# Decoding the last weights inside the last product of a three-layer kernel, and adding one product straight from PSUM

## The chip, the cores and the metric

The kernel runs on one core of one Trainium2 chip. The core has five engines that each run their own program in order: TensorE (PE, matmuls), VectorE (DVE), ScalarE (ACT), GpSimd (POOL) and SyncE (SP), which here only issues transfers (DMA). They meet at semaphores. The metric is the device time of one execution in microseconds (us), the median of three runs; lower is better.

## The reference

All data are fp32. An attention with a small memory is followed by two layers on 2304 tokens of 512 values:

```
a    = softmax(phi, over the sequence)                    # 32 memory rows per head
k_m, v_m = a^T k, a^T v
attn = softmax(q k_m^T / sqrt(64)) v_m                    # 4 batches, 8 heads, 576 x 64
x    = attn as 2304 x 512
x    = ((x @ w_a) * (x @ w_b)) @ w_out                    # 512 -> 1536 -> 512
h    = x @ moe2_w_in                                      # 512 -> 2048
out  = (h * sigmoid(1.702 h)) @ moe2_w_out                # 2048 -> 512
```

## The kernel before

**Numbers.** A product in full fp32 is made of three passes of a faster form: each operand is split into a high part (a copy to fp32r, on ACT, L281) and the rest (a subtraction on POOL or DVE, L275), by `hi_lo`; the passes are high x high, low x high, high x low.

**Weights arrive as 64-bit numbers** and are decoded on the chip. Sixteen pieces of `w_in` and sixteen chunks of `w_out` of the last layer, 128 rows of 512 values each, come as raw words of 512 KB into one of two buffers `raw` (L307). `decode_piece` makes one step on ACT (`Abs`, L379), a maximum on DVE or POOL (L381) and three steps on DVE (L385, L389, L394) into one of the decode buffers `dm`; the last of them gives the raw buffer back, and SP may then load the next piece into it. DVE reads the raw words in the last two steps.

**The last layer's first product** is computed by seven products instead of eight (P1 to P7, each on sums and differences of quarters of the operands) for each of 24 pairs of a group of 256 features `g` (8) and a group of 768 tokens `p` (3). The code calls such a pair a `quad`. One product is 6 matmuls of 128x384 (L1046) into one of eight PSUM banks. The results are put together in the SBUF tile `acc`: P1 and P5 are copied there by ACT (`kept`, L1081), P6, P2, P7, P3 and P4 are added from PSUM by DVE to something in `acc` (`added`, L1088), and two sums that hold P5 are made from two SBUF tiles by POOL or DVE (`paired`, L275). The four blocks that come out go through the gelu on ACT (L1105) and are written to DRAM, `g2d` (L1107).

**The last product** (`proj2`, L1174) has 18 token tiles of 128, each with 16 chunks of the contraction and three passes: 864 matmuls of 128x512. It reads the gelu's results back, 384 tokens and half of the contraction at a time (`load_gated`, L1139, 1536 KB), splits them into tiles `sb`, and sums a token tile over two halves of 8 chunks in one bank. The weights for it are chunks decoded between the quads, written to DRAM as fp32 (`w2d`, L408), read back when there is room for their split form (`load_chunk`, L1120) and split then (`split_chunk`).

**What sets the order.** `Order` runs all these generators against simulated clocks of the four engines, with a price for each operation, a priority for each stream and a model of the transfers, and so writes one fixed program for each engine; SP's program is in the order in which the generators issue transfers. Pieces are decoded in the order of the list `pieces`: two pieces of `w_in` per feature group and, from the third group on, three chunks of `w_out` behind them. At run time each engine follows its program, and an instruction that waits holds up all that stand behind it on its engine.

## Time and profile before

| | us |
|---|---|
| median of 3 runs | 840.15 (839.57 to 840.37) |
| the profiled execution, as a run | 842.18 |
| its span in the trace | 840.4 |
| PE busy | 801.4 |
| DVE busy | 554.4 |
| ACT busy | 396.3 |
| POOL busy | 345.3 |

The mean granted clock of TensorE was 0.942 of 2.4 GHz. In the trace the attention lies in the first 100 us, the middle layer runs from there to about 434, the quads of the last layer from about 415 to 636, and the last product from 636 to 835.7. A row of a window gives an engine's busy time in a stretch and, in brackets, the number of its instructions; a row of a group gives count, busy time and mean duration of one form of instruction, then how long the engine stood idle ahead of such instructions and what ended that. A timeline row has the idle time ahead of an instruction in square brackets, with what ended it.

### The profile page before, as it was taken

To read this page: it belongs to the slowest core of one execution; us is meant where nothing else is said; L and a number is where in the kernel's file an instruction comes from. 1 tells how busy PE (TensorE), PEld (TensorE's weight loads), DVE (VectorE), ACT (ScalarE), POOL (GpSimd) and SP (SyncE) were. 2 spreads that over 40 slices of the span, in tenths; PEclk is the share of its full clock that TensorE was granted. 3 is DMA by queue.
4 is the path that set the end of the run, shared out by engine and by line. 5 is a ranking of instruction groups with operands and counts; after the bars stand their busy time and mean duration, and the time that the engine had idled before them with its cause. 6 is when DMAs were issued, how large, how long until landed. Compare 5 with 4: busy or idle time off the path is not lost. (4 is left out here: it accounts for less than half of the span.)

```text
span 840.4 us, 13393 instructions
## 1 busy us (share of the span) xinstructions
PE 801.4 (95%) x4928; PEld 706.5 (84%) x4928; DVE 554.4 (66%) x965; ACT 396.3 (47%) x863; POOL 345.3 (41%) x327
## 2 busy tenths in 40 slices
PE   8989999989999999999988898788999999999997
PEld 7768888889889999999887897777998888888886
DVE  4979879997978778648999778689665212222120
ACT  4567767454555445426564445444574322222210
POOL 1314244653546335226998777567555000000000
PEclk9999999999999999999898999899999999999999
DMA  8776302321311303000124446776469523343201
GB/s 307 264 232 192 99 1 76 101 76 51 100 52 51 101 2 100 25 2 1 60 92 130 155 151 218 258 241 214 150 218 317 180 91 109 105 159 114 90 23 37
DMA packets 63937, 103.89 MB, mean 124 GB/s; under 512 B 5760, under 2 KB 42624, under 8 KB 63872
## 3 DMA queue, kind: packets, MB, share of 16 engines
q1 hardware_dynamic: 63040, 102.23, 37.4%
q10 hardware_dynamic: 832, 0.82, 0.3%
q8 instruction: 38, 0.62, 0.3%
q14 instruction: 27, 0.22, 0.1%
HBM read 75.24 MB, written 27.79 MB: 123 GB/s over the span
## 5 line engine op out<-in xcount | busy, mean ns | idle before, releaser
L275 DVE TENSOR_TENSOR attn<-acc,attn 128x1024 fp32r<-128x1024 f32 (+1 forms) x41 | 49.4, 1208 | 125.3 <-ACT attn L281 125.3
L1174 PE MATMUL bank<-y,attn 128*128 128x512 f32 x540 | 127.8, 394 | 0.0
L1174 PEld LDWEIGHTS bank<-y,attn 128*128 128x128 f32 x540 | 101.7, 188 | 23.0
L275 POOL TENSOR_TENSOR acc<-acc 128x384 f32<-128x384 f32 (+1 forms) x64 | 76.1, 1196 | 48.4 <-DVE acc L1088 21.3
L281 ACT ACTIVATE attn<-acc 128x1024 fp32r<-128x1024 f32 (+1 forms) x48 | 43.5, 920 | 66.2 <-PE bank L1174 59.2
L1088 DVE TENSOR_TENSOR acc<-bank,acc 128x384 f32<-128x384 f32 x120 | 63.4, 548 | 12.8 <-ACT acc L1081 5.9
L1105 ACT ACTIVATE acc<-acc 128x384 f32<-128x384 f32 x96 | 46.9, 517 | 43.0 <-DVE acc L1088 39.4
L275 POOL TENSOR_TENSOR y<-gr,y 128x288 fp32r<-128x288 f32 x43 | 37.5, 871 | 70.8 <-ACT y L281 70.7
L800 DVE TENSOR_TENSOR gr<-bank,gr 128x288 f32<-128x288 f32 x96 | 43.1, 450 | 30.8 <-PE bank L784 23.1
L797 ACT ACTIVATE gr<-bank 128x288 f32<-128x288 f32 x96 | 38.1, 399 | 39.6 <-PE bank L784 35.4
L817 PE MATMUL bank<-g,whl_b 128*128 128x288 f32 x384 | 53.7, 296 | 3.2 <-POOL g L275 2.1
L784 PE MATMUL bank<-attn,eff 128*128 128x288 f32 x384 | 55.1, 297 | 1.0 <-ACT eff L755 0.7
L817 PEld LDWEIGHTS bank<-g,whl_b 128*128 128x128 f32 x384 | 51.8, 188 | 4.5 <-POOL g L275 2.6
L379 ACT ACTIVATE dm<-raw 128x512 f32<-128x512 f32 x51 | 33.8, 671 | 45.9 <-DMA raw<-in_moe_w_in_dram 18.2
L784 PEld LDWEIGHTS bank<-attn,eff 128*128 128x128 f32 x384 | 52.2, 188 | 3.1 <-issue 1.0
L275 POOL TENSOR_TENSOR g<-gr,g 128x288 fp32r<-128x288 f32 x37 | 35.4, 962 | 44.2 <-ACT g L281 44.2
L840 PE MATMUL bank<-y,whl_a 128*128 128x512 f32 (+1 forms) x240 | 52.2, 371 | 0.4 <-POOL y L275 0.4
L840 PEld LDWEIGHTS bank<-y,whl_a 128*128 128x128 f32 x240 | 41.6, 188 | 9.3 <-POOL y L275 1.2
L394 DVE SCALAR_TENSOR_TENSOR dm<-raw,dm 128x512 uint32<-128x512 uint32 x49 | 45.2, 922 | 0.3
L389 DVE SCALAR_TENSOR_TENSOR dm<-raw,dm 128x512 uint32<-128x512 uint32 x51 | 43.9, 860 | 0.5
L275 POOL TENSOR_TENSOR wab_hl<-dm,wab_hl 128x512 fp32r<-128x512 f32 (+1 forms) x30 | 34.2, 1148 | 22.8 <-ACT wab_hl L281 20.5
L784 PE MATMUL bank<-attn,eff_b 128*128 128x288 f32 x288 | 40.8, 296 | 1.3 <-DVE acc L871 1.1
(241 smaller groups left out, 1809.4 us busy)
## 6 DMA issues: line engine op xcount, KB each, us to landing
g2d<-acc SPq DMA_DIRECT2D x96, 192.0 KB, 3.2
acc<-g2d SPq DMA_DIRECT2D x12, 1536.0 KB, 6.6
raw<-in_moe_w_out_dram SPq DMA_DIRECT2D x28, 512.0 KB, 3.9
raw<-in_moe_w_in_dram SPq DMA_DIRECT2D x16, 512.0 KB, 4.2
raw<-in_moe_w_a_dram SPq DMA_DIRECT2D x20, 256.0 KB, 2.9
raw<-in_moe_w_b_dram SPq DMA_DIRECT2D x20, 256.0 KB, 3.1
q<-in_q_dram SPq DMA_DIRECT2D x8, 576.0 KB, 6.7
out_dram<-dm SPq DMA_DIRECT2D x56, 64.0 KB, 1.7
```

The lines of the kernel that those rows point to most:

```text
L275: (nc.gpsimd if e == POOL else nc.vector).tensor_tensor(out=dst, in0=in0, in1=in1, op=op)
L281: nc.scalar.activation(out=hi, in_=src, func=AF.Copy)
L389: nc.vector.scalar_tensor_tensor(out=mu, in0=hw, scalar=0xC0000000, in1=mu, op0=ALU.bitwise_and, op1=ALU.bitwise_or)
L394: nc.vector.scalar_tensor_tensor(out=dst.bitcast(U32), in0=lw, scalar=29, in1=mu, op0=ALU.logical_shift_right, op1=ALU.bitwise_or)
L784: nc.tensor.matmul(ps[0][:, :U], e[c][:, sw, i * CW + j * P:i * CW + (j + 1) * P], attn(b, mv, c, u * U, U), start=(n == 0), stop=(n == 3 ...
L797: nc.scalar.activation(out=gr[0], in_=pa_[0][:, :U], func=AF.Copy)
L800: nc.vector.tensor_tensor(out=gr[0], in0=pb[0][:, :U], in1=gr[0], op=ALU.mult)
L817: nc.tensor.matmul(ps[0][:, :U], w[:, sw, j, mb * P:(mb + 1) * P], g1[0][:, j, mv, :], start=(n == 0), stop=(n == 3 * G1 - 1),)
L840: nc.tensor.matmul(ps[0][:, :e - o], w[:, sw, j, mb * P:(mb + 1) * P], g1_all[mv][:, j, o:e], start=(n == 0), stop=(n == 3 * G1 - 1),)
L1088: nc.vector.tensor_tensor(out=s[0], in0=ps[0][:, :N2], in1=x[0], op=ALU.add)
L1105: nc.scalar.activation(out=c[0], in_=c[0], func=AF.Gelu_apprx_sigmoid)
L1174: nc.tensor.matmul(ps[s][0], b[0][:, sw, c, :], wo2[h * KH + c][:, mv], start=(h == c == n == 0), stop=(h == 1 and c == KH - 1 and n == 2),)
```

## The change

- **P5 is not copied.** The quad's order becomes P1, P6, P7, P5, P3, P4, P2, and DVE adds P5 from its bank twice, to two tiles of `acc`; `paired` is gone. Per quad ACT has one copy instead of two, DVE seven sums from PSUM instead of five, and the sums of two SBUF tiles fall away.
- **No way through DRAM for the last weights.** The sixteen chunks of `w_out` stand behind all pieces of `w_in` in the list, and `decode_piece` splits a chunk straight into its place once there is room. `w2d`, its 16 writes and 16 reads are gone. Eight chunks are decoded in the last quads, eight within the last product.
- **More decode buffers.** Two views of a tile that the attention no longer uses serve as decode buffers for the first three pieces of `w_in` (`BRIEF`) beside the one already there, and are retired before that memory is used anew.
- **The last product.** Its first two units of 384 tokens (`FRONT`; six token tiles) go by quarters of the contraction: chunks 0 to 3 for all six tiles, then 4 to 7, and so on, with six banks open; the others by halves as before. Tiles `sb` have 8 places instead of 4.

Counted in DVE's program from the first sum of the quads to the last:

| on DVE | before | after |
|---|---|---|
| sums from PSUM (L1088, after L1104) | 120 | 168 |
| decodes (their last three steps) | 27 | 18 |
| of these with the maximum on DVE | 22 | 10 |
| splits of 128x384 | 22 | 18 |
| splits of 128x256 | 14 | 1 |
| the same within the first four quads: sums / decodes / splits of 128x384 | 20 / 6 / 21 | 28 / 2 / 18 |

```diff
+    bdv_m = p2.tile([P, B * H * M], F32, name="bdv")
+    bdv = [
+        bdv_m[:, b * H * M:(b + 1) * H * M].rearrange("p (r m) -> p r m", r=H // 2) for b in range(B)
+    ]
     gr_s = slots(p2, 3, [P, U], "gr")
-    dm_x = slots(p2, 1, [P, 512], "dm_x").free[0]
-    dm_s.free.append(dm_x)
+    dm_x = slots(p2, 1, [P, 512], "dm_x").free
+    dm_s.free += dm_x
...
-    chunks = [(("o2", c), 0, [rows(w_o2, c, 1, 0, DM)], 1) for c in range(F2 // P)]
     for g in range(NG2):
         pieces += [(("in", g), i, [rows(w_in, 2 * i, 2, g * G2 * P, G2 * P)], 2) for i in range(2)]
-        for _ in range(3 if g > 1 else 0):
-            if chunks:
-                pieces.append(chunks.pop(0))
-    pieces += chunks
+    pieces += [(("o2", c), 0, [rows(w_o2, c, 1, 0, DM)], 1) for c in range(F2 // P)]
...
-            if m is dm_x and name[0] in ("in", "o2"):
-                od.mark(m[1], "dm_x")
-                m = yield "slot", dm_s
-            if name[0] == "in" and name[1] < 2:
+            if name[0] in ("in", "o2"):
+                brief, aside = (name, part) in BRIEF, []
+                while any(m is x for x in dm_x) != brief:
+                    aside.append(m)
+                    m = yield "slot", dm_s
+                dm_s.free += aside
+            if name[0] == "in" and name[1] < 3:
                 prio = PI
             elif name[0] in ("in", "o2"):
                 prio = PR
             od.spawn(prio, decode_piece(max(t, m[1]), i, name, part, n, m))
+
+    BRIEF = ((("in", 0), 0), (("in", 0), 1), (("in", 1), 0))
+
+    def retire_dm(m, t):
+        if any(m is x for x in dm_x):
+            od.mark(t, "dm_x", len(retired))
+            retired.append(m)
+        else:
+            dm_s.release(m, t)
+
+    retired = []
...
         elif name[0] == "o2":
             c = name[1]
-            nc.sync.dma_start(out=w2d[c * P:(c + 1) * P, :], in_=m[0])
-            dm_s.release(m, t + 2500.0)
-            od.mark(t + 2500.0, *name)
+            t = max(t, (yield "mark", "room", *name))
+            t = yield from hi_lo(t, wo2[c][:, HI], wo2[c][:, LO], m[0], DM)
+            dm_s.release(m, t)
+            od.mark(t, "wo2", c)
         else:
...
+        more = [[bdv_m[:, i * 512:(i + 1) * 512], t1] for i in range(2)]
+        dm_x.extend(more)
+        dm_s.free += more
...
+    def room_split(*flat):
+        give(sb_s, [x.rearrange("p (i c t) -> p i c t", i=2, c=KH) for x in flat])
...
+        room_split(*views(big["wab"], SN, 2), big["vhl"], spare())
...
+        if name == "P1":
+            od.spawn(0, kept(t, q, ps, "s"))
+        left = [len(SUMS[name])]
+        for other, out_, place in SUMS[name]:
+            od.spawn(0, added(t, q, ps, other, out_, place, left))
 
     SUMS = {
-        "P1": ("s", None, None), "P5": ("p5", None, None), "P6": ("u2", "s", None), "P2": ("c11", "s", (0, 0)),
-        "P7": ("u3", "u2", None), "P3": ("c12", "u4", (0, 1)), "P4": ("c21", "u3", (1, 0)),
+        "P1": (), "P6": (("s", "u2", None),), "P7": (("u2", "u3", None),),
+        "P5": (("u2", "u4", None), ("u3", "c22", (1, 1))), "P3": (("u4", "c12", (0, 1)),),
+        "P4": (("u3", "c21", (1, 0)),), "P2": (("s", "c11", (0, 0)),),
     }
-    USES = {"s": 2, "p5": 2, "u2": 2, "u3": 2, "u4": 1}
+    USES = {"s": 2, "u2": 2, "u3": 2, "u4": 1}
...
+    def added(t, q, ps, other, name, place, left):
         t1, x = yield from get(q, other)
         t, s = yield DVE, max(t, t1), dve(N2), hb_s
         nc.vector.tensor_tensor(out=s[0], in0=ps[0][:, :N2], in1=x[0], op=ALU.add)
-        bank_m.release(ps, t)
+        left[0] -= 1
+        if left[0] == 0:
+            bank_m.release(ps, t)
         drop(q, other, t)
-        yield from put(t, q, name, s, place)
-
-    def paired(q, one, two, name, place=None):
-        t1, x = yield from get(q, one)
-        t2, y = yield from get(q, two)
-        s = yield "slot", hb_s
-        t = yield from combine(max(t1, t2, s[1]), s[0], x[0], y[0], ALU.add, N2)
-        drop(q, one, t)
-        drop(q, two, t)
...
+    FRONT = 2
+    parts = [(i, h) for h in range(2) for i in range(FRONT)]
+    parts += [(i, h) for i in range(FRONT, len(units)) for h in range(2)]
...
+        for i, h in parts:
+            for g in range(h * n, (h + 1) * n):
+                for j in range(2):
+                    t = yield "mark", "g2", (g, i // 2), j, i % 2
+            s = yield "slot", f_s
+            f = s[0].rearrange("p (c t) -> p c t", c=KH)
+            o = units[i]
...
+    def proj2(tiles, cuts):
+
+        ps = {}
+        for o, e in cuts:
+            h = o // KH
+            for i, s in tiles:
                 t = yield "mark", "sb", i, h, s
-                if i == s == 0:
-                    for c in range(h * KH, (h + 1) * KH):
-                        t = max(t, (yield "mark", "wo2", c))
-                b = loaded.pop(("sb", i, h, s))
-                if h == 0:
-                    t, ps[s] = yield PE, t, 680 * KH, bank_m
+                for c in range(o, e):
+                    t = max(t, (yield "mark", "wo2", c))
+                b = loaded["sb", i, h, s]
+                if o == 0:
+                    t, ps[i, s] = yield PE, t, 680 * (e - o), bank_m
                 else:
-                    t, _ = yield PE, t, 680 * KH
-                for c in range(KH):
+                    t, _ = yield PE, t, 680 * (e - o)
+                for c in range(o, e):
                     for n, (mv, sw) in enumerate(PASSES):
                         nc.tensor.matmul(
-                            ps[s][0], b[0][:, sw, c, :], wo2[h * KH + c][:, mv],
-                            start=(h == c == n == 0), stop=(h == 1 and c == KH - 1 and n == 2),
+                            ps[i, s][0], b[0][:, sw, c - h * KH, :], wo2[c][:, mv],
+                            start=(c == n == 0), stop=(c == 2 * KH - 1 and n == 2),
                         )
-                sb_s.release(b, t)
-                if h == 1:
-                    od.spawn(0, proj2_out(t, units[i] // P + s, ps[s]))
+                if e % KH == 0:
+                    sb_s.release(b, t)
+                if e == 2 * KH:
+                    od.spawn(0, proj2_out(t, units[i] // P + s, ps[i, s]))
...
+        for i in range(3):
+            yield "mark", "dm_x", i
         room_projected()
         od.spawn(6, load_gated())
         od.spawn(5, split_gated())
-        for c in range(F2 // P):
-            od.spawn(6, load_chunk(c))
         for q in order[1:]:
             yield from quad(*q)
             if q == (NG2 - 1, 0):
                 room_chunks(*views(big["y0"], CN, 10))
             if q == (NG2 - 1, 1):
-                room_split()
+                room_split(*views(attn_m[0], SN, 2), *views(attn_m[1], SN, 2))
...
+        tiles = [(i, s) for i in range(len(units)) for s in range(N2 // P)]
+        n = FRONT * N2 // P
+        yield from proj2(tiles[:n], [(o, o + KH // 2) for o in range(0, 2 * KH, KH // 2)])
+        for o in range(n, len(tiles), N2 // P):
+            yield from proj2(tiles[o:o + N2 // P], [(0, KH), (KH, 2 * KH)])
 
     def quad(g, p):
-        for name in ("P1", "P5", "P6", "P2", "P7", "P3", "P4"):
+        for name in ("P1", "P6", "P7", "P5", "P3", "P4", "P2"):
```

In the orders below names are those of buffers, with the number of a tile behind some of them; line numbers of the changed kernel are its own (L1081 is L1097 there, L1088 L1104, L1105 L1114, L1107 L1116, L307 L308, L379 to L394 L390 to L405). DVE within the second and third quad before:

```order
L1088 TENSOR_TENSOR acc<-bank_76,acc 128x384
L381 TENSOR_SCALAR dm_85<-dm_85 128x512
L1088 TENSOR_TENSOR acc<-bank_71,acc 128x384
L385 TENSOR_SCALAR dm_85<-dm_85 128x512
L389 SCALAR_TENSOR_TENSOR dm_85<-raw_79,dm_85 128x512
L1088 TENSOR_TENSOR acc<-bank_74,acc 128x384
L275 TENSOR_TENSOR eff_b<-acc,eff_b 128x384
L394 SCALAR_TENSOR_TENSOR dm_85<-raw_79,dm_85 128x512
L381 TENSOR_SCALAR dm_83<-dm_83 128x512
L275 TENSOR_TENSOR g_95<-acc,whl_b 128x384
L385 TENSOR_SCALAR dm_83<-dm_83 128x512
```

and after:

```order
L1104 TENSOR_TENSOR acc<-bank_72,acc 128x384 x2
L1104 TENSOR_TENSOR acc<-bank_71,acc 128x384
L276 TENSOR_TENSOR whl_b<-acc,whl_b 128x384
L1104 TENSOR_TENSOR acc<-bank_70,acc 128x384
L276 TENSOR_TENSOR g_94<-acc,g_94 128x384
L1104 TENSOR_TENSOR acc<-bank_73,acc 128x384
L276 TENSOR_TENSOR g_94<-acc,g_94 128x384 x2
L276 TENSOR_TENSOR rest<-acc,rest 128x384
L1104 TENSOR_TENSOR acc<-bank_76,acc 128x384
L276 TENSOR_TENSOR rest<-acc,g_94 128x384
L1104 TENSOR_TENSOR acc<-bank_74,acc 128x384
```

The steps of two decodes (L381 to L394) stood between the sums; now sums and splits (L275, after L276) alternate.

ACT in the middle of the quads, before:

```order
L1081 ACTIVATE acc<-bank_75 128x384
L1081 ACTIVATE acc<-bank_77 128x384
L379 ACTIVATE dm_84<-raw_80 128x512
L1105 ACTIVATE acc<-acc 128x384
L379 ACTIVATE acc<-raw_79 128x512
L1105 ACTIVATE acc<-acc 128x384 x3
L1081 ACTIVATE acc<-bank_78 128x384
L1081 ACTIVATE acc<-bank_75 128x384
L379 ACTIVATE dm_83<-raw_80 128x512
L1105 ACTIVATE acc<-acc 128x384
L379 ACTIVATE dm_85<-raw_79 128x512
```

and after:

```order
L282 ACTIVATE wab_hl<-dm_82 128x256
L1114 ACTIVATE acc<-acc 128x384
L282 ACTIVATE wab_hl<-dm_82 128x256
L1114 ACTIVATE acc<-acc 128x384
L282 ACTIVATE wab_hl<-dm_83 128x256
L1114 ACTIVATE acc<-acc 128x384 x2
L1097 ACTIVATE acc<-bank_77 128x384
L390 ACTIVATE dm_82<-raw_79 128x512
L390 ACTIVATE dm_83<-raw_78 128x512
L1114 ACTIVATE acc<-acc 128x384 x4
L1097 ACTIVATE acc<-bank_73 128x384
```

Steps of a decode (L379) came every one to four instructions, between copies (L1081) and gelus (L1105). Now two of them (L390) stand together, and no others for a group's worth of gelus and splits (L282).

SP in the middle of the quads, before:

```order
L1107 DMA g2d<-acc 128x384 x3
L408 DMA w2d<-dm_85 128x512
L307 DMA raw_79<-in_moe_w_out_dram 128x1024
L1107 DMA g2d<-acc 128x384
L408 DMA w2d<-dm_84 128x512
L307 DMA raw_80<-in_moe_w_in_dram 128x2x512
L1107 DMA g2d<-acc 128x384 x3
L1139 DMA acc<-g2d 128x8x384
L408 DMA w2d<-dm_85 128x512
L307 DMA raw_79<-in_moe_w_in_dram 128x2x512
L1107 DMA g2d<-acc 128x384
```

and after:

```order
L1116 DMA g2d<-acc 128x384
L308 DMA raw_79<-in_moe_w_in_dram 128x2x512
L1116 DMA g2d<-acc 128x384 x3
L308 DMA raw_78<-in_moe_w_in_dram 128x2x512
L1116 DMA g2d<-acc 128x384 x9
L308 DMA raw_79<-in_moe_w_out_dram 128x1024
L1116 DMA g2d<-acc 128x384 x3
L308 DMA raw_78<-in_moe_w_out_dram 128x1024
L1116 DMA g2d<-acc 128x384 x9
L308 DMA raw_79<-in_moe_w_out_dram 128x1024
L1116 DMA g2d<-acc 128x384 x3
L308 DMA raw_78<-in_moe_w_out_dram 128x1024
```

A load of raw words stood behind a write of a decoded chunk (L408); now it stands among the gelu's writes to `g2d` alone.

## Rows read from the trace of the kernel before

**Rows 1.** The page, busy time of engines (us, share of span, instructions)
```profile
PE 801.4 (95%) x4928; PEld 706.5 (84%) x4928; DVE 554.4 (66%) x965; ACT 396.3 (47%) x863; POOL 345.3 (41%) x327
```

**Rows 2.** Windows: length, busy us and count of PE, PEld, DVE, ACT, POOL; clock, DMA
```profile
406.10:470.00 63.90, 54.95 (x294) 50.26 (x293) 63.34 (x94) 33.26 (x73) 57.71 (x50) 0.88 0.36 113
470.00:605.40 135.40, 121.37 (x640) 110.48 (x638) 101.45 (x170) 67.01 (x154) 90.64 (x88) 0.94 0.60 201
605.40:636.00 30.60, 30.59 (x175) 30.60 (x176) 20.66 (x30) 20.97 (x42) 20.15 (x17) 0.95 0.69 222
636.00:835.70 199.70, 199.65 (x865) 162.28 (x863) 45.69 (x38) 48.75 (x60) 8.12 (x6) 0.95 0.37 120
```

**Rows 3.** Windows, line L1046 alone: length, PE, PEld, clock, DMA share, GB/s
```profile
406.10:470.00 63.90, 41.80 (x196) 37.44 (x197) 0.88 0.36 113
470.00:605.40 135.40, 121.37 (x640) 110.48 (x638) 0.94 0.60 201
605.40:636.00 30.60, 30.59 (x174) 30.30 (x174) 0.95 0.69 222
```

**Rows 4.** Groups of instructions, PE, 406.1 to 470: count, busy us, mean ns, idle before
```profile
L817 PE MATMUL bank<-g,whl_b 128*128 128x288 f32 x50 | 7.5, 299 | 2.1 <-POOL g L275 2.1
L784 PE MATMUL bank<-attn,eff_b 128*128 128x288 f32 x48 | 6.5, 294 | 0.0
```

**Rows 5.** Groups of instructions, DVE, 406 to 636
```profile
L1088 DVE TENSOR_TENSOR acc<-bank,acc 128x384 f32<-128x384 f32 x118 | 62.4, 548 | 10.9 <-ACT acc L1081 5.9 <-ACT y L281 2.6 <-PE bank L1046 1.8
L394 DVE SCALAR_TENSOR_TENSOR dm<-raw,dm 128x512 uint32<-128x512 uint32 x22 | 21.0, 953 | 0.1
L389 DVE SCALAR_TENSOR_TENSOR dm<-raw,dm 128x512 uint32<-128x512 uint32 x21 | 19.3, 918 | 0.2
L385 DVE TENSOR_SCALAR dm<-dm 128x512 uint32<-128x512 uint32 x21 | 13.7, 652 | 4.0 <-POOL dm L381 3.6
L381 DVE TENSOR_SCALAR dm<-dm 128x512 f32<-128x512 f32 x19 | 13.2, 697 | 14.3 <-ACT dm L379 13.9 <-POOL vhl L275 0.4
L275 DVE TENSOR_TENSOR attn<-acc,attn 128x384 fp32r<-128x384 f32 x7 | 7.9, 1128 | 0.0
L275 DVE TENSOR_TENSOR wab_hl<-dm,wab_hl 128x256 fp32r<-128x256 f32 x4 | 2.8, 704 | 1.2 <-ACT wab_hl L281 1.2
```

**Rows 6.** Groups of instructions, ACT, 406 to 636
```profile
L1081 ACT ACTIVATE acc<-bank 128x384 f32<-128x384 f32 x48 | 21.9, 477 | 2.1 <-POOL y L275 1.6 <-PE bank L1046 0.5
L379 ACT ACTIVATE dm<-raw 128x512 f32<-128x512 f32 x20 | 13.3, 666 | 28.5 <-DMA raw<-in_moe_w_in_dram 18.2 <-DMA raw<-in_moe_w_out_dram 10.2
```

**Rows 7.** Groups of instructions, POOL, 406 to 636
```profile
L275 POOL TENSOR_TENSOR acc<-acc 128x384 f32<-128x384 f32 x57 | 68.3, 1204 | 48.4 <-DVE acc L1088 21.3 <-issue 16.4 <-ACT acc L1081 6.1
L381 POOL TENSOR_SCALAR acc<-acc 128x512 f32<-128x512 f32 x3 | 5.2, 1722 | 0.7 <-DVE dm L394 0.6
```

**Rows 8.** Timeline of ACT: start, us, engine, line, operation [idle before]
```profile
499.88 0.66 ACT L379 ACTIVATE dm<-raw 128x512 f32<-128x512 f32 x1 [3.90 <-DMA raw<-in_moe_w_out_dram]
500.44 0.51 ACT L1105 ACTIVATE acc<-acc 128x384 f32<-128x384 f32 x1
```

**Rows 9.** Timeline of PE
```profile
501.98 1.33 PE L1046 MATMUL bank<-eff_b,wab_hl 128*128 128x384 f32 x6 [1.01 <-DVE acc L1088]
```

**Rows 10.** Timeline of SP (issues of transfers)
```profile
493.82 0.32 SPq L408 DMA_DIRECT2D w2d<-dm  x1
494.19 0.42 SPq L307 DMA_DIRECT2D raw<-in_moe_w_out_dram  x1
```

**Rows 11.** DMA issues, 440 to 636: engine, count, size, median us to landing
```profile
raw<-in_moe_w_out_dram SPq DMA_DIRECT2D x13, 512.0 KB, 4.2
raw<-in_moe_w_in_dram SPq DMA_DIRECT2D x10, 512.0 KB, 4.9
acc<-g2d SPq DMA_DIRECT2D x2, 1536.0 KB, 7.2
```

More of the change, by code (lines that the diff above doesn't have):

```diff
@@ L25 @@
 PR = 30
-PB2 = 5
 MBN = 8
@@ L236, in tile_mem_attention_moe_moe2 @@
     p2 = tc.alloc_tile_pool(name="p2", bufs=1)
-    bdv = [p2.tile([P, H // 2, 2 * M], F32, name=f"bdv{b}") for b in range(B)]
+    bdv_m = p2.tile([P, B * H * M], F32, name="bdv")
+    bdv = [
+        bdv_m[:, b * H * M:(b + 1) * H * M].rearrange("p (r m) -> p r m", r=H // 2) for b in range(B)
+    ]
     gr_s = slots(p2, 3, [P, U], "gr")
-    dm_x = slots(p2, 1, [P, 512], "dm_x").free[0]
-    dm_s.free.append(dm_x)
+    dm_x = slots(p2, 1, [P, 512], "dm_x").free
+    dm_s.free += dm_x
     ident = pa.tile([P, P], F32, name="ident")
@@ L1030, in combine_weights @@
         for x in m:
-            dm_s.release(x, t)
+            retire_dm(x, t)
     sums = {}
@@ L1113, in tile_mem_attention_moe_moe2 @@
     units = list(range(0, NT, N2))
-    def load_chunk(c):
-        t = yield "mark", "room", "o2", c
-        t = max(t, (yield "mark", "o2", c))
-        m = yield "slot", dm_s
-        nc.sync.dma_start(out=m[0], in_=w2d[c * P:(c + 1) * P, :])
-        od.load(max(t, m[1]), P * DM * 4, "chunk", c)
-        od.spawn(PB2, split_chunk(c, m))
-    def split_chunk(c, m):
-        t = yield "mark", "chunk", c
-        t = yield from hi_lo(t, wo2[c][:, HI], wo2[c][:, LO], m[0], DM)
-        dm_s.release(m, t)
-        od.mark(t, "wo2", c)
+    FRONT = 2
@@ L1145, in split_gated @@
-    def split_gated():
-        for i in range(len(units)):
-            for h in range(2):
-                t = yield "mark", "f", i, h
-                slot, f = loaded.pop(("f", i, h))
-                for s in range(N2 // P):
-                    b = yield "slot", sb_s
-                    t2 = yield from hi_lo(
-                        max(t, b[1]), b[0][:, HI], b[0][:, LO], f[:, :, s * P:(s + 1) * P], KH * P
-                    )
-                    loaded["sb", i, h, s] = b
-                    od.mark(t2, "sb", i, h, s)
-                f_s.release(slot, t2)
@@ L1159, in proj2 @@
-    def proj2(i):
-        ps = [None] * (N2 // P)
-        for h in range(2):
-            for s in range(N2 // P):
-                t = yield "mark", "sb", i, h, s
-                if i == s == 0:
-                    for c in range(h * KH, (h + 1) * KH):
-                        t = max(t, (yield "mark", "wo2", c))
-                b = loaded.pop(("sb", i, h, s))
-                if h == 0:
-                    t, ps[s] = yield PE, t, 680 * KH, bank_m
-                else:
-                    t, _ = yield PE, t, 680 * KH
-                for c in range(KH):
+        for i, h in parts:
[5 more added lines that the diff above has]
+            o = units[i]
+            nc.sync.dma_start(
+                out=f, in_=g2d[h * KH * P:(h + 1) * KH * P, o:o + N2].rearrange("(c p) t -> p c t", p=P)
+            )
+            od.load(max(t + 2500.0, s[1]), KH * P * N2 * 4, "f", i, h)
+            loaded["f", i, h] = s, f
```

35 lines of the change are left out of this document (9 added, 26 removed).

## The prediction

> **What bounds the kernel now.** I read the page first: TensorE (PE) is busy 801.4 us, 95% of the span [rows 1], so with these matmuls no more than 840.4 - 801.4 = 39.0 us of idle can be had. Where do they lie? I cut the span into stretches and read, for each, the busy time of every engine [rows 2], and the matmuls of the first product of the last layer alone [rows 3]. From 605.4 to 636.0 PE has no gap: 174 of these matmuls in 30.59 us, 175.8 ns each. One unit of the work there, called a quad below (a feature group with a token group, seven products of 6 matmuls), therefore costs 42 x 175.8 ns = 7.38 us when nothing holds it up. Held against that price:
> - 406.1 to 470.0: 196 x 0.1758 = 34.5 us, and the rest of the layer before, 6.5 + 7.5 [rows 4]: 48.5 of 63.9 us, 15.4 lost.
> - 470.0 to 605.4: 640 x 0.1758 = 112.5 of 135.4 us, 22.9 lost.
> - 605.4 to 636.0, and the last product to 835.7: nothing lost. Behind it stands a tail of 840.4 - 835.7 = 4.7 us.
>
> (These 38.3 us contain matmuls that ran slowly behind a gap, which the page counts as busy.) The two places have two causes. In the first, VectorE (DVE) works 63.34 of 63.90 us, a plain limit of throughput [rows 2]. In the second it works 101.45 of 135.40 us and is no limit by its sum. There the latency of loads counts. ScalarE (ACT) runs in order, and stands before its step of a decode (L379) for 28.5 us, all of it until raw words have landed [rows 6]; before the step at 499.88 it stood 3.90 us [rows 8]. Behind that step in its queue are the copies of P1 and P5 (L1081) and the gelus; DVE's sums need the copies, PSUM banks come free through these sums, and PE then stood 1.01 us before 501.98 on such a sum [rows 9]. Why are the words late? SyncE (SP) issues in order, and the raw load stands right behind the write of a decoded chunk (L408), which waits for the end of that chunk's decode: write at 493.82, load at 494.19, step at 499.88 [rows 8, 10]. A raw load takes 4.2 to 4.9 us to land [rows 11]; ACT's wait is that latency, exposed.
>
> **The change part by part.** The sum goes against the profiled run, 842.18 us (span 840.4 and 1.78 around it), which is 2.03 above the median of 840.15.
>
> *P5 from PSUM.* ACT loses one of two copies per quad, 21.9 / 2 = 11 us [rows 6]; POOL (GpSimd) loses sums of two SBUF tiles, at most 48 x 1.204 = 57.8 us [rows 7]; DVE gains 48 adds, 48 x 0.548 = 26.3 us, of a kind that stands 118 times in the trace [rows 5]. P5's bank is held for two adds instead of one copy, some 0.6 us more; with eight banks at 7.38 / 7 = 1.05 us a product, PE has seven products, 7 us, before it misses one. I take 0 for that; where DVE is that far behind, the cover is gone and it costs 0.6 x 24 = 14 us.
>
> The Trainium skill, "VectorE: DVE Perf Modes", section "Rules for kernel authors", speaks against this edit: it offers a copy from PSUM to SBUF first when a matmul's output gets many operations. Its errata table would make an add from PSUM (120 + 384) / 0.96 = 525 ns, an estimate; the trace has 548. What the rule would mean here is my second rival.
>
> *Decoding.* A decode is one step on ACT, a maximum on DVE or POOL, and three steps on DVE: 0.652 + 0.918 + 0.953 = 2.52 us, with the maximum 0.697 more [rows 5]. In DVE's order there are 27 decodes (22 with the maximum) between the first sum of the quads and the last, and after the change 18 (10): eight chunks have gone behind the quads, one ahead of them. That takes off 9 x 2.52 + 12 x 0.697 = 31.0 us; 13 splits of 128x256 and 4 of 128x384 go too, 13 x 0.704 + 4 x 1.128 = 13.7 us [rows 5]. DVE's balance over the quads is 26.3 - 31.0 - 13.7 = -18.4 us, of 63.34 + 101.45 + 20.66 = 185.5.
>
> *First stretch (406.1 to 470.0).* It holds the first four quads. Within them DVE's decodes fall from 6 to 2, its splits of 128x384 from 21 to 18, its sums rise from 20 to 28: -4 x (2.52 + 0.697) - 3 x 1.128 + 8 x 0.548 = -11.9 us of 63.3. That leaves DVE 51.4, only 3 us above PE's 48.5, and two engines that wait for each other never meet exactly. POOL, 57.71 of 63.90 busy, loses 8 sums, 9.6 us. I take **-10**. Ends: -3 (the stretch stays as long as POOL's present 57.71 and 5% for order, 60.6) and -15.4 (nothing lost).
>
> *Middle (470.0 to 605.4).* All pieces of the first weight are now decoded ahead of the chunks of the second, two per three quads, and there are two raw buffers; no write to memory stands on SP's way to the next load. A load is issued about three quads (22 us) before its step on ACT and lands in 4.9 [rows 11], so the 28.5 us of ACT's waits go. DVE's load per quad there: 7 x 0.548 + 12/17 x (2.52 + 0.35) = 5.86 us, 79% of 7.38, where it has 5 x 0.548 + 21/17 x (2.52 + 0.53) + 0.50 (splits) = 7.0 now, 95% (12 and 21 decodes in 17 quads; half, and 16 of 21, with the maximum). Late next is DVE in the last five quads, into which eight chunks are put: 3.84 + 1.6 x 2.87 = 8.4 us a quad, 1.0 over, 5 us; and one more for sums that stand behind a decode. So 22.9 lost become 6: **-17**. Ends: -8 (only the waits for chunks, 10.2 of 28.5 us, go: 22.9 x 10.2 / 28.5) and -22.9.
>
> *Ahead of it.* PE's order up to the first quad is as it was; one piece more is decoded, 3.2 us of DVE, beside matmuls. Cost 0, ends -1 and +3.
>
> *Last product.* The same 864 matmuls, 199.65 us [rows 2], the first six token tiles by quarters of the contraction: a quarter of a tile is 12 x 199.65 / 864 = 2.77 us, of six tiles 16.6. So chunks 8 to 11 are wanted 33 us and 12 to 15 50 us after its start. A pair of chunks costs in series 4.2 (load) + 0.67 + 1.72 (maximum on POOL) + 2 x 2.52 = 11.6 us [rows 5 to 7, 11], the last four pairs 46 us. SP issues their first load ahead of the last quads' end, so they are ready some 25 to 44 us after the start, 6 ahead of need. The six tiles need two loads of 1536 KB at 7.2 us [rows 11]; the first split out of the second is ready some 4 us before PE wants it. DVE works 45.69 and ACT 48.75 of 199.70 us here [rows 2]; eight decodes add 8 x 2.87 = 23 us to DVE. If this cover is gone, PE waits for what is late. Cost 0, ends -0.5 and +8. The tail is as before.
>
> **Sum:** 842.18 - 10 - 17 = 815.2 for such a run, 813.2 on the median's side; I put **814**.
>
> **Rivals.** (1) *Only part of the waits goes.* The first stretch is ruled by the chain weight sum, ACT's split, POOL's split, not by DVE. For it: POOL has 90% there. Against: DVE has 99%. Then -3, and -13 in the middle, halfway between its end and my value: **824**. (2) *DVE becomes the bound of all quads*, since P5 is read twice from PSUM by the engine that is already the fullest. Per quad it has (185.5 - 18.4) / 24 = 6.96 us, 94% of 7.38; if in each quad 1.2 us are lost to order, as in the middle now (22.9 us in 640 / 42 = 15.2 quads is 1.5), 24 x 1.2 = 29 of the 38 us stay lost: **831**. Against: now the waits come from ACT, and those go. (3) *The end starves: slower.* The last chunks pass two raw buffers, whose next load waits for DVE's last step of a decode, with splits of 128x1024 and ACT's own waits ahead of it in both queues. If a pair takes 20 us instead of 11.6, four take 80, chunks 12 to 15 come 30 us late and the 27 us are more than given back: **843**. It decides from 19 us a pair on. For it: ACT does stand 4 us before a single load [rows 8]. Against: in the last product both engines are three quarters idle. (4) *The change does not do what it says*: ACT's waits come back with the chunks wherever these stand and DVE's -18 us are not on the path: **840**. Against: a gap of PE that begins with a wait of ACT for a load [rows 8, 9].
>
> **How the numbers follow.** Forecast (804 to 821) 0.60; rival 1 0.18; rival 2 0.11; rival 3 0.06; rival 4 0.05, half of it within 0.2%, which is 1.7 us and about what a measurement of this kernel can tell from no change. The range goes from 804, where all but 2 us of the 38.3 are regained, to 830, which leaves out rivals 3 and 4 and half of rival 2. Faster 0.60 + 0.18 + 0.11 + 0.01 = 0.90, same 0.03, slower 0.07.
>
> **What would show it.** Right: the quads end near 609 instead of 636; ACT's waits for raw words in the quads are under 5 us; DVE is under 90% in the middle, near 100% only in the first and the last quads; PE has no gap behind the start of the last product. Wrong: gaps of PE before a sum from PSUM in every quad (rival 2); a first stretch as long as before with POOL full (rival 1); PE waiting in the last product for a split chunk or a token tile (rival 3).

## The result and the profile after

806.39 us (806.17 to 807.11, 4 runs) against 839.86 (838.44 to 840.37, 4 runs): ratio 0.9606, 95% interval 0.9589 to 0.9622, 33.5 us less. The forecast was 814, range 804 to 830. (The median of before has one run more here than the one given above.)

The page of the kernel after, in the columns of [rows 1]; its span is 804.4 us:

```profile
PE 782.6 (97%) x4928; PEld 703.0 (87%) x4928; DVE 552.6 (69%) x983; ACT 386.6 (48%) x839; POOL 318.8 (40%) x309
```

PE lost 18.8 us of busy time although it runs the same matmuls, and idles 21.8 us where it idled 39.0. Some 5 us of the 18.8 belong to the run and not to the change: in a second look at the kernel before, PE is busy 796.4 us. The other 13.8 fell away with the gaps: at the same clock of 1.00 quads 6 to 18 keep PE busy for 104.14 us (547 matmuls) in that second look and for 95.43 (549) in the kernel after, as the rows below show. Of the gaps few are left.

The profile of before shown above is of a run whose granted clock was 0.95 outside its slow stretches; a second profile of the kernel before (the last experiment below) and the kernel after had 1.00 there. I compare these two, by the same work. Windows of the kernel before, second look, columns as in [rows 2]: quads 1 to 5 with the rest of the layer before, quads 6 to 18, quads 19 to 24, last product:

```profile
405.50:471.80 66.30, 56.03 (x309) 51.47 (x308) 64.13 (x95) 34.41 (x76) 59.41 (x51) 0.95 0.37 118
471.80:590.20 118.40, 104.14 (x547) 92.99 (x546) 90.21 (x149) 57.85 (x134) 79.51 (x76) 1.00 0.64 208
590.20:635.30 45.10, 44.78 (x253) 43.86 (x254) 30.80 (x49) 28.66 (x60) 28.96 (x26) 1.00 0.59 192
635.30:833.70 198.40, 198.40 (x865) 162.21 (x864) 45.61 (x38) 48.69 (x60) 8.32 (x6) 1.00 0.37 121
```

The kernel after, by the same work:

```profile
404.20:461.80 57.60, 52.51 (x308) 50.77 (x307) 54.15 (x89) 30.84 (x67) 45.73 (x40) 0.97 0.23 77
461.80:557.50 95.70, 95.43 (x549) 95.11 (x548) 69.54 (x126) 47.65 (x111) 46.21 (x60) 1.00 0.53 179
557.50:601.40 43.90, 43.90 (x254) 43.90 (x253) 35.86 (x60) 25.28 (x51) 24.61 (x20) 1.00 0.48 157
601.40:799.90 198.50, 198.45 (x865) 161.92 (x863) 63.23 (x66) 55.24 (x72) 28.74 (x17) 1.00 0.41 134
```

The stretches took 66.3, 118.4, 45.1 and 198.4 us; they take 57.6, 95.7, 43.9 and 198.5. The first quad begins 1.3 us earlier on PE (404.2 for 405.5), and the tail is 0.2 shorter. So: 8.7 us from the first five quads, 23.9 from the other nineteen, nothing from the last product; with the start and the tail 34.0 in all, the difference of the spans (838.4 - 804.4). Of the 8.7 us, 7.8 lie in quads 2 to 5: the second quad begins at 434.7 in the kernel before and at 432.6 in the kernel after, so that these four take 37.1 and 29.2 us. From the second quad on PE has one gap of 0.27 us up to 601.4.

The rows of the kernel after that answer to [rows 6], groups of ACT from 404 to 602:

```profile
L1097 ACT ACTIVATE acc<-bank 128x384 f32<-128x384 f32 x24 | 11.4, 474 | 0.0
L390 ACT ACTIVATE dm<-raw 128x512 f32<-128x512 f32 x13 | 8.2, 662 | 2.4 <-DMA raw<-in_moe_w_in_dram 2.4
```

Those that answer to [rows 5], groups of DVE:

```profile
L1104 DVE TENSOR_TENSOR acc<-bank,acc 128x384 f32<-128x384 f32 x163 | 84.5, 549 | 32.8 <-PE bank L1062 18.3 <-ACT acc L1097 11.7 <-ACT acc L390 1.6
L405 DVE SCALAR_TENSOR_TENSOR dm<-raw,dm 128x512 uint32<-128x512 uint32 x13 | 11.5, 882 | 0.2
L400 DVE SCALAR_TENSOR_TENSOR dm<-raw,dm 128x512 uint32<-128x512 uint32 x13 | 9.9, 760 | 0.2
L396 DVE TENSOR_SCALAR dm<-dm 128x512 uint32<-128x512 uint32 x13 | 8.2, 628 | 1.1 <-POOL dm L392 0.9
```

And the sums on POOL, as in [rows 7]:

```profile
L276 POOL TENSOR_TENSOR acc<-acc 128x384 f32<-128x384 f32 x15 | 18.4, 1244 | 0.5 <-DVE acc L276 0.5
```

ACT's wait for raw words in the `dm` buffers fell from 28.5 to 2.4 us. DVE's add from PSUM costs what it cost, 549 for 548 ns, 163 times for 118 in the window. POOL's sums fell from 57 to 15. Idle of DVE before its sums is now mostly a wait for PE (18.3 us): PE sets the pace.

What is left in the quads lies in the first. PE's timeline of the kernel after, idle time in brackets:

```profile
408.27 5.76 PE L1062 MATMUL bank<-y,wab_hl 128*128 128x384 f32 x31 [1.34 <-POOL y L276]
421.63 0.53 PE L832 MATMUL bank<-g,whl_b 128*128 128x288 f32 x2 [1.25 <-ACT g L282]
423.86 0.72 PE L832 MATMUL bank<-g,whl_b 128*128 128x288 f32 x3 [1.69 <-POOL g L276]
424.92 7.78 PE L832 MATMUL bank<-g,whl_b 128*128 128x288 f32 x43 [0.34 <-POOL g L276]
```

The last product's last chunk shows how near the other side was. SP's timeline of the kernel after, loads of raw words (L308) and of token tiles (L1137), several in one row where it says x2 or more, with the time from the first to the last:

```profile
600.89 3.11 SPq L308 DMA_DIRECT2D raw<-in_moe_w_out_dram  x2
610.72 1.00 SPq L1137 DMA_DIRECT2D acc<-g2d  x2
613.65 17.74 SPq L308 DMA_DIRECT2D raw<-in_moe_w_out_dram  x4
```

ACT, its step of the chunk loaded at 613.65 and its part of the split of chunk 15 (`eff_b`):

```profile
623.62 0.66 ACT L390 ACTIVATE dm<-raw 128x512 f32<-128x512 f32 x1 [3.45 <-DMA raw<-in_moe_w_out_dram]
651.24 0.63 ACT L282 ACTIVATE eff_b<-acc 128x512 fp32r<-128x512 f32 x1 [3.38 <-DVE acc L405]
```

POOL, the other part of that split:

```profile
651.95 1.29 POOL L276 TENSOR_TENSOR eff_b<-acc,eff_b 128x512 fp32r<-128x512 f32 x1 [2.48 <-ACT eff_b L282]
```

PE, the first matmuls with chunk 15:

```profile
652.94 1.08 PE L1170 MATMUL bank<-eff_b,vhl 128*128 128x512 f32 x3
```

The last decode ends at about 651.2, its split on POOL at 651.95 + 1.29 = 653.24, and PE's first matmuls with that chunk start at 652.94 (its high part; the low part is wanted by the third of them). There is no time to spare: the three matmuls take 1.08 us where three with the next token tile take 0.85, so PE already lost 0.2 us, though the timeline shows no gap. The rows also show where the time went: the raw load of 613.65 stands behind two loads of 1536 KB, issued at 610.72, and ACT's step gets its words 10 us later, at 623.62; such a load took 4.2 us in [rows 11].

### The profile page after: what moved, and what is told of

It reads as the page before. It is cut to its first block, busy times and chain, and to the rows that moved or that the text cites. A ratio compares the mean times of both kernels' runs of the same rounds, so it can differ in the third digit from the quotient of the medians.

```text
span 804.4 us, 13239 instructions
## 1 busy us (share of the span) xinstructions
PE 782.6 (97%) x4928; PEld 703.0 (87%) x4928; DVE 552.6 (69%) x983; ACT 386.6 (48%) x839; POOL 318.8 (40%) x309
## 5 line engine op out<-in xcount | busy, mean ns | idle before, releaser
L1104 DVE TENSOR_TENSOR acc<-bank,acc 128x384 f32<-128x384 f32 x168 | 86.9, 549 | 32.8 <-PE bank L1062 18.3
L1114 ACT ACTIVATE acc<-acc 128x384 f32<-128x384 f32 x96 | 48.1, 520 | 55.2 <-DVE acc L1104 54.9
L1170 PE MATMUL bank<-y,attn 128*128 128x512 f32 x300 | 70.8, 391 | 0.0
L1170 PEld LDWEIGHTS bank<-y,attn 128*128 128x128 f32 x300 | 56.3, 188 | 12.3
L276 POOL TENSOR_TENSOR y<-gr,y 128x288 fp32r<-128x288 f32 x43 | 37.7, 879 | 63.9 <-ACT y L282 63.7
L832 PE MATMUL bank<-g,whl_b 128*128 128x288 f32 x384 | 55.6, 302 | 4.3 <-POOL g L276 2.0
L832 PEld LDWEIGHTS bank<-g,whl_b 128*128 128x128 f32 x384 | 53.3, 193 | 6.0 <-POOL g L276 2.8
L276 DVE TENSOR_TENSOR attn<-acc,attn 128x1024 fp32r<-128x1024 f32 (+1 forms) x24 | 28.8, 1202 | 39.6 <-ACT attn L282 39.6
L276 POOL TENSOR_TENSOR g<-gr,g 128x288 fp32r<-128x288 f32 x37 | 35.6, 967 | 44.4 <-ACT g L282 44.1
L276 POOL TENSOR_TENSOR wab_hl<-dm,wab_hl 128x256 fp32r<-128x256 f32 (+1 forms) x31 | 29.3, 955 | 38.7 <-ACT wab_hl L282 36.4
L282 ACT ACTIVATE y<-gr 128x288 fp32r<-128x288 f32 x48 | 21.3, 444 | 43.5 <-DVE gr L815 43.3
L875 DVE TENSOR_TENSOR acc<-bank,acc 128x512 f32<-128x512 f32 (+1 forms) x72 | 37.9, 548 | 5.1 <-PE bank L855 4.5
L799 PEld LDWEIGHTS bank<-attn,eff_b 128*128 128x128 f32 x288 | 39.0, 188 | 2.4 <-DVE acc L886 1.6
L390 ACT ACTIVATE dm<-raw 128x512 f32<-128x512 f32 x41 | 26.9, 667 | 23.5 <-DMA raw<-in_moe_w_b_dram 11.7
L392 POOL TENSOR_SCALAR dm<-dm 128x512 f32<-128x512 f32 x17 | 27.3, 1610 | 26.9 <-ACT dm L390 26.0
```

The lines of the kernel that those rows point to most:

```text
L276: (nc.gpsimd if e == POOL else nc.vector).tensor_tensor(out=dst, in0=in0, in1=in1, op=op)
L392: (nc.vector if e == DVE else nc.gpsimd).tensor_scalar(out=mf, in0=mf, scalar1=2.0 ** -15, scalar2=None, op0=ALU.max)
L799: nc.tensor.matmul(ps[0][:, :U], e[c][:, sw, i * CW + j * P:i * CW + (j + 1) * P], attn(b, mv, c, u * U, U), start=(n == 0), stop=(n == 3 ...
L832: nc.tensor.matmul(ps[0][:, :U], w[:, sw, j, mb * P:(mb + 1) * P], g1[0][:, j, mv, :], start=(n == 0), stop=(n == 3 * G1 - 1),)
L875: nc.vector.tensor_tensor(out=dst, in0=ps[0][:, a - o:z - o], in1=dst, op=ALU.add)
L1104: nc.vector.tensor_tensor(out=s[0], in0=ps[0][:, :N2], in1=x[0], op=ALU.add)
```

## Experiments

There are two theories on the middle. **L** says that the idle time was the latency of raw loads, exposed by the order of the pieces and by the write ahead of them on SP. **S** says that it was the path of the sums, that is ACT's copy of P5 and POOL's sums of two SBUF tiles. Two pairs of kernels tell them apart: each part alone in the kernel before, and each undone in the kernel after. Times below are medians; "before" on the same chips was 838.7 to 839.3. Three points in a diff stand for lines left out.

**P5 copied again** (in the kernel after; the order of the seven products goes back with it):

```diff
-        "P5": (("u2", "u4", None), ("u3", "c22", (1, 1))),
+        "P5": ("p5", None, None),      # kept() by ACT, paired() twice, as before
...
-        for name in ("P1", "P6", "P7", "P5", "P3", "P4", "P2"):
+        for name in ("P1", "P5", "P6", "P2", "P7", "P3", "P4"):
```

> The changed kernel with P5 copied by ScalarE again, its two sums made from SBUF tiles by GpSimd or VectorE and the old order of the seven products; all else as changed. Theory L (the idle time of the middle quads was the latency of raw loads, exposed by the order of the pieces and the write on SyncE's queue): the middle stays without loss, only the first four quads lose 3 to 5 us: 809 to 812 us. Theory S (the idle time came from the sums, that is the copy of P5 on ScalarE and the pair sums on GpSimd): most of the gain goes, 822 us or more.

Measured: **808.98** us (808.82 to 809.39), ratio to before 0.9644 (0.9628 to 0.9661). Windows, quads 1 to 5 and 6 to 24:

```profile
404.20:463.50 59.30, 53.73 (x308) 51.49 (x308) 54.69 (x84) 32.36 (x71) 51.59 (x45) 0.94 0.22 75
463.50:602.40 138.90, 138.90 (x800) 138.90 (x799) 99.25 (x169) 78.23 (x178) 96.90 (x92) 1.00 0.52 172
```

The other nineteen quads have no gap with P5 copied: 138.90 of 138.90 us. The first five took 59.3 for 57.6, and the last product lost 1.9 (in this profile the nineteen take 0.7 less). Theory S falls.

**P5 from PSUM alone** (in the kernel before, the reverse of that diff).

> The kernel before with one part of the change alone: P5 added twice from PSUM, new order of the seven products. Theory L: the waits of ScalarE for raw words stay, 835 to 837 us. Theory S: 818 to 822 us.

Measured: **836.92** us (834.28 to 839.59), ratio 0.9978 (0.9961 to 0.9994): 2.1 us, with runs that overlap those of before. ACT from 406 to 631, to be held against [rows 6]:

```profile
L379 ACT ACTIVATE dm<-raw 128x512 f32<-128x512 f32 x20 | 13.4, 671 | 35.9 <-DMA raw<-in_moe_w_in_dram 23.1 <-DMA raw<-in_moe_w_out_dram 10.0 <-DVE acc L871 1.6
```

The waits for raw words are still there (23.1 + 10.0 of the 35.9 us), with half the copies behind them. P5, with the order of the products, is worth 2 to 3 us in either kernel.

**The list's order alone** (in the kernel before):

```diff
-        for _ in range(3 if g > 1 else 0):
-            if chunks:
-                pieces.append(chunks.pop(0))
```

> The kernel before with one part alone: all pieces of the first weight are decoded ahead of the sixteen chunks of the second; the chunks still go through DRAM and the last product still goes by halves. Theory L: the quads end at 612 us or earlier instead of 636, and what is won is lost again behind them, since all chunks come late: 825 to 845 us in all. Theory S: the quads end at 628 us or later.

Measured: **846.73** us (845.97 to 848.02), ratio 1.0097 (1.0082 to 1.0112): slower. Windows: quads 6 to 18, 19 to 24, last product:

```profile
466.70:562.75 96.05, 95.94 (x548) 94.74 (x547) 64.56 (x117) 51.65 (x123) 66.68 (x68) 1.00 0.54 176
562.75:614.40 51.65, 47.41 (x254) 43.08 (x254) 41.83 (x65) 27.93 (x59) 33.83 (x28) 1.00 0.81 261
614.40:840.30 225.90, 206.71 (x865) 164.59 (x863) 61.00 (x62) 55.96 (x74) 19.99 (x14) 0.93 0.40 129
```

The quads ended at 614.4, 2 us later than theory L had it, and the whole is 2 us above its range. Quads 6 to 18 took 96.05 us, as in the kernel after (95.7) and 22 less than before: that loss was the list's order. The last product took 225.9 instead of 198.4: the won time went back with interest, since all chunks came late and the second half wanted eight at once.

This order takes two things out of these quads, the raw loads of the chunks and the work of their decodes: DVE has 64.56 us to do there instead of 90.21. So the run alone does not tell theory L from a rival, that DVE had too much to do. The trace of the kernel before speaks for L. The chain that ended last, followed back at each step to what released it, goes from 494 to 563 through five raw loads, 29.1 us in all; the first is that of [rows 10], the others are:

```profile
523.22 5.81 DMA raw<-in_moe_w_in_dram
531.57 7.49 DMA raw<-in_moe_w_in_dram
547.06 4.82 DMA raw<-in_moe_w_out_dram
557.31 5.41 DMA raw<-in_moe_w_in_dram
```

SP stood 31.2 us (ten times, from 440 to 636) before writes of decoded chunks until DVE's last step of their decode:

```profile
SPq L408 <- DVE dm L394: 31.2, 10, 7.4
```

How much the work alone may cost is seen in the kernel with 96 more adds below. There DVE has 78.13 us in 465 / 42 = 11.1 quads, 7.1 each, where the kernel before has 90.21 in 13.0, 6.9 each. PE takes 90.0 / 11.1 = 8.1 us a quad there, 0.8 over the 7.3 of the kernel after; before it took 118.4 / 13.0 = 9.1, 1.8 over. So less than half of the loss would be the work, if adds weigh like decodes. No run separates the two further.

**Halves instead of quarters** (in the kernel after):

```diff
-    FRONT = 2
+    FRONT = 0
```

> The changed kernel with every token tile of the last product by halves of the contraction, none by quarters. In the changed kernel chunk 15 is split at 653 us, 0.4 us after TensorE wants it. By halves the first token tile wants chunks 8 to 15 from 618 us on. If the chunks' chain sets its own pace: 25 to 32 us lost, 831 to 838 us. If the chain goes faster when nothing else runs: 815 to 822 us.

Measured: **835.93** us (834.57 to 836.96), ratio 0.9963 (0.9950 to 0.9976). The quads end at 601.2, as with quarters. PE at the second half of the first tile:

```profile
630.11 0.79 PE L1170 MATMUL bank<-g,attn 128*128 128x512 f32 x1 [10.78 <-ACT g L282]
636.95 0.79 PE L1170 MATMUL bank<-g,attn 128*128 128x512 f32 x1 [2.55 <-ACT g L282]
```

The window of the stall, columns as in [rows 2]:

```profile
618.70:660.00 41.30, 20.25 (x48) 12.05 (x47) 23.37 (x27) 13.35 (x20) 14.74 (x9) 0.59 0.53 176
```

PE waits for one chunk after another: 21.0 us of gaps (41.30 - 20.25), and a granted clock of 0.59 in this stretch, in which the few matmuls between them run slowly as well (0.42 us each for 0.23). Without the quarters nearly the whole gain is given back; what the prediction's third rival feared for the changed kernel is what happens here.

**Chunks through DRAM** (in the kernel after):

```diff
-            t = max(t, (yield "mark", "room", *name))
-            t = yield from hi_lo(t, wo2[c][:, HI], wo2[c][:, LO], m[0], DM)
+            nc.sync.dma_start(out=w2d[c * P:(c + 1) * P, :], in_=m[0])   # and load_chunk, split_chunk
...
```

> The changed kernel, but each chunk of the second weight is written to DRAM after its decode and read back before its split, as before; quarters, list order and P5 as changed. In the changed kernel the last chunk has no time to spare (its split ends 0.3 us after TensorE is ready for it). Theory L: the write (2.2 us) and the read (3.2 us) lengthen the chain of the last chunks, and the next raw load stands behind a waiting write again: 5 to 15 us lost, in the last quads and the last product, 811 to 821 us. Rival (transfers are hidden anyway): 806 to 808 us.

Measured: **816.87** us (814.73 to 818.95), ratio 0.9732 (0.9711 to 0.9753). Windows: quads 19 to 24, last product:

```profile
558.80:610.40 51.60, 45.88 (x255) 43.53 (x254) 40.22 (x67) 26.67 (x54) 27.83 (x22) 1.00 0.76 249
610.40:812.50 202.10, 199.54 (x865) 161.66 (x863) 62.55 (x64) 53.77 (x70) 21.32 (x12) 1.00 0.44 144
```

The last six quads took 51.6 for 43.9, the last product 202.1 for 198.5. The way through DRAM costs 10.5 us by the medians.

**48 and 96 additional adds on DVE** (in the kernel after; the sums of P6 and P7 computed twice or three times):

```diff
+        k = 2 if name in ("u2", "u3") else 1      # 3 in the second kernel
...
+        for _ in range(k):
             nc.vector.tensor_tensor(out=s[0], in0=ps[0][:, :N2], in1=x[0], op=ALU.add)
```

> The changed kernel with 48 additional adds from PSUM on VectorE: the sums of P6 and P7 are each computed twice into the same tile (26 us of VectorE over the quads, 1.0 us a quad; VectorE then has some 6.8 of 7.3 us a quad in the middle). If the prediction's second rival has the right rule (an engine at 94% costs TensorE 1.2 us a quad): 20 us or more lost, 826 us. If eight banks hide it as long as the sum stays under TensorE's: 0 to 4 us lost, in the first four and the last five quads, 806 to 810 us.

> The changed kernel with 96 additional adds from PSUM on VectorE: the sums of P6 and P7 are each computed three times (53 us over the quads, 1.9 us a quad at the pace of 0.47 us, 7.7 of 7.3 us a quad in the middle, more in the last five). VectorE is then the bound: 10 to 25 us lost, 816 to 831 us. If the other edge is reached earlier than by the sums, more.

Measured: **813.72** us (813.18 to 814.58) and **827.95** (826.17 to 828.97). The first misses both expectations, and most of its cost lies outside the places named. The second lies within what was expected. Windows of the quads with 48:

```profile
470.00:560.00 90.00, 90.00 (x519) 90.00 (x518) 74.08 (x139) 43.48 (x100) 45.73 (x56) 1.00 0.53 178
560.00:602.80 42.80, 42.80 (x247) 42.80 (x246) 37.05 (x68) 24.86 (x51) 22.55 (x20) 1.00 0.47 156
```

PE in the last product with 48:

```profile
624.87 7.36 PE L1172 MATMUL bank<-y,attn 128*128 128x512 f32 x24 [1.36 <-POOL y L276]
```

DVE works 82% of 470 to 560 and 87% of 560 to 602.8, and PE has no gap there. The first quad took 1.7 us more, and the last product 5.6 more (204.1 us): the chain that had nothing to spare stalls PE, at 624.87 for a split of a chunk. With 96:

```profile
470.00:560.00 90.00, 84.66 (x465) 83.05 (x464) 78.13 (x150) 41.52 (x97) 47.09 (x59) 0.96 0.48 162
560.00:617.00 57.00, 54.00 (x298) 52.93 (x297) 52.05 (x100) 25.91 (x56) 26.41 (x23) 0.97 0.43 145
```

DVE is at 87% and 91%, and now PE has gaps: 5.3 of 90 and 3.0 of 57 us; one quad, which waits for its weights (3.3 of the 5.3), takes 13.9 us for 7.3. So with such adds the edge lies between 82 and 87% in the middle and between 87 and 91% in the last six quads, and below it a loaded DVE costs PE nothing in the quads. The load of the second rival, 94% of a quad's 7.38 us, is reached only with the 96 adds (7.1 us), and there the loss is 0.8 us a quad where it took 1.2.

**What holds the first quad?** Four kernels, from the kernel after. The third group's pieces decoded later:

```diff
+            if name == ("in", 2):
+                t = max(t, (yield "mark", "s", (1, 0)))
```

> The changed kernel, but the decode of the pieces of the third feature group starts when the second quad has begun, instead of within the first; nothing else. In the changed kernel the only loss left in the quads is some 5 us between 406 and 425 us, where VectorE is full (33.9 of 34 us) and its sums of the layer before (L815) stand behind steps of two decodes. If these steps are the cause: 2 to 4 us faster, 802 to 804 us. If GpSimd's splits of that stretch are: 806 us.

Measured: **811.45** us (811.23 to 811.72), 5 us slower, outside both expectations. The window of the gaps in the kernel after and in this one, then PE's timeline in this one:

```profile
404.00:425.00 21.00, 16.02 (x99) 14.52 (x97) 20.93 (x36) 11.88 (x25) 20.73 (x20) 0.99 0.19 64
404.00:425.00 21.00, 16.52 (x99) 14.71 (x97) 20.59 (x35) 11.14 (x25) 20.39 (x20) 0.97 0.11 39
472.83 0.45 PE L1064 MATMUL bank<-y,wab_hl 128*128 128x384 f32 x1 [1.56 <-ACT wab_hl L282]
474.43 7.91 PE L1064 MATMUL bank<-y,wab_hl 128*128 128x384 f32 x35 [1.16 <-POOL wab_hl L276]
```

PE's gaps are hardly smaller without the decodes' steps (4.5 us for 5.0), and the seventh quad now waits for its weights. But `Order` has put other work in the place of these steps, three sums of two SBUF tiles among it, and DVE is as full as it was (20.59 for 20.93 of 21.00 us). So these steps as such were not the cause; that a full DVE is, this run does not exclude. The second quad moved up:

```diff
         room_gated()
+        yield from quad(1, 0)
         yield from proj(g, 3, 0)
...
```

> The changed kernel with the second quad (feature group 1, token group 0) moved up in TensorE's order, ahead of the last 96 matmuls L832 of the layer before. Those wait for splits of the gelu-free product g (idle of 1.25, 1.69 and 0.34 us before them at 421 to 425 us, and 3.4 us at half clock behind it); the quad's operands are split by 417 us. If the stall is the latency of that chain: 3 to 5 us faster, 801 to 803 us. If VectorE and GpSimd are bound by their sums there (33.9 and 33.1 of 34 us): the wait comes again at a later quad of that stretch, 805 to 808 us.

Measured: **804.59** us (803.91 to 804.75), ratio 0.9584 (0.9568 to 0.9600). All its runs lie below those of the changed kernel (806.17 and more), but the two were not run in turn on one chip and the intervals of their ratios overlap, so that a gain of some 2 us is likely and not shown. PE:

```profile
432.74 1.06 PE L832 MATMUL bank<-g,whl_b 128*128 128x288 f32 x6 [1.40 <-DVE acc L1104]
435.76 3.44 PE L832 MATMUL bank<-g,whl_b 128*128 128x288 f32 x24 [0.69 <-DVE acc L1104]
```

The gaps before L832 that waited for `g` are gone, others of 1.40 and 0.69 us wait for DVE's sums, and no stretch of the quads has a low clock. It looks as if a part of the loss was latency that other work can cover, while the rest comes back as a wait for DVE's sums. The second quad one step earlier still, ahead of the last `gated`:

> As the one before, but the second quad stands between the last two groups of 24 matmuls L799, so that the first half of that product's chain has 7.3 us and the second none. If latency: 2 to 4 us faster, 802 to 804 us; if bound by sums: 805 to 808 us.

Measured: **806.70** us (805.60 to 806.89), no gain, as the reading by sums had it. And one brief buffer instead of three:

```diff
-    BRIEF = ((("in", 0), 0), (("in", 0), 1), (("in", 1), 0))
+    BRIEF = ((("in", 0), 1),)
...
```

> The changed kernel with one brief decode buffer as before instead of three. One piece of the second feature group is then decoded within the first quads instead of ahead of them (3.2 us of VectorE in a stretch where it is full). If VectorE binds that stretch: 2 to 4 us slower, 808 to 811 us. If the chains through GpSimd do: within 1 us, 806 to 807 us.

Measured: **811.31** us (810.94 to 811.99): 4.9 us slower, a little more than the larger figure expected.

```profile
410.20 0.79 PE L1062 MATMUL bank<-y,wab_hl 128*128 128x384 f32 x3 [3.77 <-POOL y L276]
429.25 8.72 PE L832 MATMUL bank<-g,whl_b 128*128 128x288 f32 x43 [1.21 <-DVE g L276]
```

From the first quad's start to the second's it took 33.0 us for 28.3, with the longest gap before POOL's split of a token operand. One decode more in this stretch delays what stands behind it; whether through DVE or POOL is not settled, as both are full there (in the kernel after 20.93 and 20.73 of 21.00 us).

**The kernel before, second look.**

> The kernel before, unchanged, for a second look at its profile. The profile shown had a granted clock of 0.95 outside three stretches at 0.50; the changed kernel and the variants of the kernel before had 1.00 outside such stretches. If that level belongs to the run and not to the kernel: 1.00 here, the last product 198.5 us instead of 199.7, a span of 837 to 838.5 us, and the same stretches at 0.50 near 410, 458 and 543 us. If it belongs to the kernel: 0.95 again.

Measured: 840.21 us, span 838.4, clock 1.00 outside two stretches at half clock (at 411 and 428 us; none at 458 and 543, where the expectation had them). So the level of 0.95 or 1.00 differs between two runs of one kernel, and the last product takes 1.3 us less at 1.00.

## Why the prediction was right, and where it was off

- *What bounds it.* Right in the main: the loss lay in two stretches, and the list's order alone took 22 us out of the middle. The chain through the raw loads speaks for ACT's waits for them as the larger part there; a smaller part can be the work of the decodes on DVE, which the prediction put at no limit by its sum. The signs named came: the quads ended at 601.4, ACT's waits for raw words fell to 2.4 us in the `dm` buffers, DVE has 73% of the middle (69.54 of 95.70 us).
- *P5 from PSUM*: 0 on the path, with DVE's balance to pay. Measured: 2.1 us gained in the kernel before, 2.6 lost when undone in the kernel after (by the profiles 1.7 in the first five quads and 1.9 in the last product, with 0.7 back between them). The Trainium skill, "VectorE: DVE Perf Modes", section "Rules for kernel authors", offers a copy out of PSUM first where many operations follow; with P5 copied it was 2.6 us slower here (808.98 for 806.39). One copy on ACT at 474 ns and two sums on POOL at 1.2 us [rows 7] were more than two adds from PSUM at 549 ns. Two operations were not many.
- *First stretch*: -10. Measured -8.7, and -1.3 ahead of it, where the prediction had 0 and an end of -1. It worked with VectorE's sum alone. Nearly all of the gain lies in quads 2 to 5. What is left, some 5 us in the first quad, stands before splits by POOL and ACT, the chain that the first rival named. The extra decode buffers (4.9 us) were counted only as one decode less.
- *Middle*: -17, measured -23.9, the step that was mis-sized. The prediction left 6 us, of which 5 because DVE would be 1.0 us over in each of the last five quads, at 8.4 us a quad. They run at 7.3 us, and DVE works 6.4 us a quad in them:

```profile
564.90:601.40 36.50, 36.50 (x212) 36.50 (x211) 32.05 (x53) 20.75 (x39) 17.85 (x11) 1.00 0.52 166
```

  Two things made the term too large. Only five of the eight chunks end their decode in these quads; two did so at 550, in the middle, and one at 602, behind them. And my price of a decode's three steps, 2.52 us, came from a trace in which POOL worked 67% of the middle (90.64 of 135.40 us); they took 0.628 + 0.760 + 0.882 = 2.27 us in the kernel after, where POOL works 48% (46.21 of 95.70). Even 87% of DVE in the last six quads left PE no gap in the kernel with 48 more adds.
- *Last product*: 0, measured +0.1, but by luck: "6 ahead of need" was -0.3 for chunk 15, and PE lost 0.2. The first load of the last four pairs went out at 600.89, as the product began and not ahead of it, and the four pairs took 52 us for 46 (600.89 to 653.24). These 6 us are what one load took above its price, 10 us where the prediction had 4.2 for every load. It was issued 3 us behind two loads of token tiles; that these slowed it is not tested.
- *Rivals.* The first (824) did not come: the first stretch won 8.7 us and not 3, the middle more than forecast. The second did not come: over all quads DVE has (54.15 + 69.54 + 35.86) / 24 = 6.6 us and not 6.96, in the middle only 5.3 (69.54 in 13.1 quads), and such a share costs PE nothing there, as the additional adds show. The third shows in the case with halves (835.93), so its mechanism is real, and the quarters are what kept it off. The fourth (840) did not come, as ACT's waits did not come back.
